# Maxout as b + relu(a-b), with the second weight cast while it loads and the early order rewritten, in a fused attention and maxout kernel

## Chip, cores and metric

The kernel runs on one core of one Trainium2 chip. The time is device microseconds of one launch, from host arrays of float32 to a float32 output. Five engines work side by side: TensorE (PE, its weight loads as PEld), VectorE (DVE), ScalarE (ACT), GpSimd (POOL) and SyncE (SP). DMAs are issued from the queues of SP, ACT and POOL.

## The reference

```python
scores = (1 / sqrt(64)) * q @ k.T          # 8 batches, 8 heads, 576 tokens, 64 wide
scores = where(block_of(row) >= block_of(col), scores, -1e9)   # blocks of 64 tokens
attn = exp(scores - max) / (sum + 1e-9)
x = (attn @ v), heads side by side          # 4608 tokens x 512
y = maximum(x @ w1, x @ w2) @ w_out         # 512 -> 1024 -> 512
```

## The kernel before, in words

All matrix work is in bfloat16. The heads are taken in pairs (p = 0 to 31, four pairs to a batch), and two pairs make a group g (q and k of a group are loaded together by `load_qk`, lines 112 to 124, cast to bf16 by `cast`, turned on TensorE by `transposes`, lines 354 to 372). Scores of a pair stand transposed, keys on partitions; `exp` (line 402) is one ScalarE instruction that reads a score buffer in PSUM, of which there are two, and writes bf16 to `aT`. `mask` (line 407) zeroes the corners on the block diagonal, mostly on GpSimd. `av` (line 471) multiplies by v with a column of constants beside it, so that the sum of the exps comes out too, and VectorE divides (lines 493 and 494) into `xp`. `x_out` (line 511) turns the result into `xT` by TensorE and two copies; from the third batch on, `x_dma` (line 502) does so by a transposing DMA.

The maximum is split: max(x w1, x w2) = (x(w1+w2) + |x(w1-w2)|) / 2. The constant beside v is 2, which halves x. The difference `d_sb` (`diff_w`, line 161) gives h by `h_unit` (line 212): four matmuls for 128 columns of d_ff and a span of tokens, then an absolute-value reduction on VectorE into `g`. The sum `s_sb` (`sum_w`, line 165) is turned by `sT_unit` (line 233) and multiplied with w_out by `m_unit` (line 245) into the small matrix `m_sb`, so that y = x m + |h| w_out has 4 + 8 matmuls for 128 tokens (`y_unit`, line 263). The weights come in four blocks of 256 columns, in float32, by `load_w` (line 148) on GpSimd's queue: the first two into buffers of their own, the last two into those of q and k. w_out is cast to bf16 as it is loaded (`load_wo`, line 171), and so is v (`load_v`, line 134).

The order is written out by hand, and each engine's queue follows the text of the program. Up to the fourth pair (lines 573 to 664) each instruction group stands by itself; from group 2 on a loop (line 673) takes one group after another. `load_qk(..., gated=True)` writes one column of the buffer on GpSimd first, so that a load on SP's queue begins when GpSimd reaches that place. The matrix work of the second half (h, sT, M and y units) stands in one list of steps; `fill(n)` (line 338) takes steps of a summed cost n off it and `fill_of` (line 542) shares what is ready among the groups. A span of h is ready when `x_out` has set `done_tokens`. The first spans have 256 and 320 tokens, the others 512. `warm_up` runs matmuls on zeros.

On GpSimd's queue the early order before the change is: cast of the third q, masks of pair 0, weight block 2, cast of the third k (line 627), masks of pair 1, weight block 3 and both halves of w_out (lines 633 to 635), masks of pair 2, three loads of v of batch 1, the key copies `pad_keys` of pairs 4 and 5, the gates of the loads of group 3, masks of pair 3, the other loads of v, and the casts of group 3. The sums and differences stand between the divisions of the `av` calls on VectorE.

Of the kernel before, what the change touches and what calls it, by code (L numbers as in the profile page):

```python
# [14 lines left out]
def kernel(  # L15
# [10 lines left out]
    nc = tc.nc  # L26
# [54 lines left out]
    small = ctx.enter_context(tc.tile_pool(name="small", bufs=4))  # L81
    xpool = ctx.enter_context(tc.tile_pool(name="xp", bufs=3))
    raw = ctx.enter_context(tc.tile_pool(name="raw", bufs=3))
    wraw = ctx.enter_context(tc.tile_pool(name="wraw", bufs=2))
    qkn = ctx.enter_context(tc.tile_pool(name="qkn", bufs=2))
    g_pool = ctx.enter_context(tc.tile_pool(name="g", bufs=2))
    y_pool = ctx.enter_context(tc.tile_pool(name="y", bufs=4))
# [11 lines left out]
    aT_r = [ring.tile([P, 2, AW + APAD], BF16, name=f"aT{r}") for r in range(NA)]  # L99
    xT = ring.tile([P, NDM, NTOK + BLK], BF16, name="xT")  # L100
    d_sb = wpool.tile([P, NDM, d_ff], BF16, name="d_sb")
    sT_sb = wpool.tile([P, NFF, d_model], BF16, name="sT_sb")
    m_sb = wpool.tile([P, NDM, d_model], BF16, name="m_sb")
    wo_sb = wpool.tile([P, NFF, d_model], BF16, name="wo_sb")
    ident = wpool.tile([P, P], BF16, name="ident")
# [20 lines left out]
    def cast(nm, g, parts):  # L126
        t = raws[nm, g].rearrange("p s (t d) -> p t s d", d=D)
        if (nm, g) not in qk_n:
            qk_n[nm, g] = qkn.tile([P, RPP, 2, D], BF16, name=f"{nm}n")
        n = qk_n[nm, g]  # L130
        for copy, j0, j1 in parts:
            copy(out=n[:, j0:j1], in_=t[:, j0:j1])  # L132

    def load_v(b, c):
        rows = min(P, S - c * P)
        nc.gpsimd.dma_start(  # L136
            out=vv_r[b % NV][P - rows:, c, :, :D],
            in_=v[b, :, c * P:c * P + rows, :].rearrange("h p d -> p h d"),
        )
# [3 lines left out]
    wor = moe_w_out.rearrange("(c p) f -> p c f", p=P)  # L143

    WB = 256
    w_raws = {}

    def load_w(j, which=(0, 1)):
        for i in which:
            if j < 2:  # L150
                t = wraw.tile([P, NDM, WB], FP32, name=f"w{i + 1}raw")[:]
            else:
                t = raw.tile([P, 2, RPP * D], FP32, name="qk"[i] + "raw").rearrange(
                    "p a b -> p (a b)")[:, :NDM * WB].rearrange("p (c f) -> p c f", c=NDM)
            w_raws[j, i] = t
            nc.gpsimd.dma_start(out=t, in_=(w1r, w2r)[i][:, :, j * WB:(j + 1) * WB])

    s_sb = g_pool.tile([P, NFF, SPAN + BLK], BF16, name="g").rearrange(
        "p f t -> p (f t)")[:, :NDM * d_ff].rearrange("p (c f) -> p c f", c=NDM)

    def diff_w(j):
        fs = slice(j * WB, (j + 1) * WB)
        nc.vector.tensor_sub(d_sb[:, :, fs], w_raws[j, 0], w_raws[j, 1])  # L163

    def sum_w(j):
        fs = slice(j * WB, (j + 1) * WB)
        nc.vector.tensor_add(s_sb[:, :, fs], w_raws[j, 0], w_raws[j, 1])

    WH = d_model // 2

    def load_wo(i):
        ds = slice(i * WH, (i + 1) * WH)
        nc.gpsimd.dma_start(out=wo_sb[:, :, ds], in_=wor[:, :, ds])  # L173
# [11 lines left out]
    load_qk(2, (SP, None))  # L185
    make_identity(nc, ident)
    for r in range(NV):
        nc.vector.memset(vv_r[r][:, :, :, D:D + 1], 2.0)
        nc.vector.memset(vv_r[r][:BLK, NCH - 1, :, :], 0.0)
    for r in range(NA):  # L190
        nc.vector.memset(aT_r[r][:, :, AW:], 0.0)
# [11 lines left out]

    done_tokens = [0]
    g_tiles = {}

    def ABS(out, in_):
        nc.vector.tensor_reduce(  # L208
            out=out, in_=in_.unsqueeze(2), op=mybir.AluOpType.max,
            axis=mybir.AxisListType.X, apply_absolute_value=True)  # L210

    def h_unit(i, f):
        if f == 0:
            g_tiles[i] = g_pool.tile([P, NFF, SPAN + BLK], BF16, name="g")
            if carry[i]:
                end = carry[i - 1] + spans[i - 1][1]
                nc.gpsimd.tensor_copy(  # L217
                    out=g_tiles[i][:, :, :carry[i]],
                    in_=g_tiles[i - 1][:, :, end - carry[i]:end])
        g = g_tiles[i]  # L220
        t0, w = spans[i]
        m = carry[i]
        pt = ps_m.tile([P, SPAN], FP32, name="ps_h", tag="m")
        for c in range(NDM):
            nc.tensor.matmul(  # L225
                pt[:, :w], d_sb[:, c, f * P:(f + 1) * P], xT[:, c, t0:t0 + w],
                start=(c == 0), stop=(c == NDM - 1),
            )
            if c == NDM - 1:
                ABS(g[:, f, m:m + w], pt[:, :w])  # L230
            yield

    def sT_unit(j):
        pt = ps_m.tile([P, 2, NDM, P], BF16, name="ps_sT", tag="m")
        for i in range(2):
            f = 2 * j + i
            for c in range(NDM):
                nc.tensor.transpose(pt[:, i, c, :], s_sb[:, c, f * P:(f + 1) * P], ident[:])
                if i == 1 and c == NDM - 1:
                    (dve if j % 2 else act)(  # L240
                        out=sT_sb[:, 2 * j:2 * j + 2, :],
                        in_=pt.rearrange("p i c d -> p i (c d)"))
                yield

    def m_unit(i, c):
        ds = slice(i * WH, (i + 1) * WH)
        pt = ps_m.tile([P, WH], FP32, name="ps_M", tag="m")
        for f in range(NFF):
            nc.tensor.matmul(  # L249
                pt[:], sT_sb[:, f, c * P:(c + 1) * P], wo_sb[:, f, ds],  # L250
                start=(f == 0), stop=(f == NFF - 1),
            )
            if f == NFF - 1:
                (act, dve)[c % 2](out=m_sb[:, c, ds], in_=pt[:])  # L254
            yield

    def y_terms(i, s):
# [38 lines left out]
    def plan():  # L296
        def h(i, f):
            t0, w = spans[i]
            units.append((h_unit(i, f), t0 + w, w / SPAN, NDM))

        def y(i, s, last=False):
            t0, w = spans[i]
            if last:
                units.append((y_last(i, s), t0 + w, 0.333, 3 * NY))
            else:
                units.append((y_unit(i, s), t0 + w, 1.0, NY))

        for i in range(NSPAN):
            for f in range(NFF):
                h(i, f)  # L310
                if i == 0 and f == NFF - 1:
                    for n in range(NFF // 2):
                        units.append((sT_unit(n), 0, 0.3, 2 * NDM))
                if i > 2 and f % 2 == 0 and f // 2 < tiles[i - 1]:
                    y(i - 1, f // 2)
            if i == 1:
                for n in range(2 * NDM):
                    units.append((m_unit(n // NDM, n % NDM), 0, 0.5, NFF))
                for j in range(2):
# [101 lines left out]
    def burst_q1(p):  # L421
        burst(p, ((0, QCUT, 320), (1, QCUT, 192)), 384)
# [151 lines left out]

    LOW = (0, -(-QCUT // RPP))
    HIGH = (LOW[1], NP)
    warm_up(16)
# [44 lines left out]
    cast("q", 2, ((pool, 0, RPP),))  # L624
    masks_q(0)
    load_w(2)
    cast("k", 2, ((pool, 0, RPP),))
    burst_q2(1)
    x_out(1, 0, 2)
    warm_up(2)  # L630
    burst_q3(1)
    masks_q(1)
    load_w(3)
    load_wo(0)
    load_wo(1)
    fill(4)
    burst_q1(2)
    transposes("q", 2, (dve, act))()
    burst_q2(2)
    av(0, [2, 3, 4])  # L640
    diff_w(1)
    burst_q3(2)
    masks_q(2)
    for c in range(3):
        load_v(1, c)
    av(1, [2, 3, 4])
    sum_w(0)
    fill(4)
    burst_q1(3)
    transposes("k", 2, (dve, act))()  # L650
    pad_keys(4)
    pad_keys(5)
    load_qk(3, (SP, SP), gated=True)
    x_out(0, 2, NCH)
    diff_w(2)
    burst_q2(3)
    av(2, [2, 3, 4])
    sum_w(1)
    burst_q3(3)
    masks_q(3)  # L660
    for c in range(3, NCH):
        load_v(1, c)
    cast("q", 3, ((pool, 0, RPP),))
    cast("k", 3, ((pool, 0, RPP),))

    x_due = []

    def av_with(p, n):
        av(p, [0, 1])
        fill(n)  # L670
        av(p, [2, 3, 4])

    for g in range(GPB, NG):
        a, b = 2 * g, 2 * g + 1
        if x_due:
            x_out(x_due.pop())
        n = fill_of(g)
        region(tile_0(a), tile_1(a))
        if g == GPB:
            av(3, [2, 3, 4])  # L680
            fill(4)
            diff_w(3)
            x_out(1, 2, NCH)
            sum_w(2)
            sum_w(3)
            fill(4)
            n = fill_of(g)
        lo, hi = max(3, n // 18), n * 2 // 9
        for p, tiles in ((a, lambda: (tile_2(a), tile_0(b))), (b, lambda: (tile_1(b), tile_2(b)))):
            fill(hi)  # L690
            if g > GPB:
                av_with(p - LAG, lo)
                if p % 2 and x_by_dma(g - 1):
                    x_dma(g - 1)
            else:
                fill(lo)
# [8 lines left out]
        if g > GPB:  # L705
            x_due.append(g - 1)
        fill(n - 2 * (lo + hi))
    for p in range(NPAIR - LAG, NPAIR):
        if x_due:
# [43 lines left out]
```

## Time and profile before

| | |
|---|---|
| time, median of 13 runs | 272.3 us (270.1 to 274.76) |
| profiled execution: time, span | 272.3 us, 270.5 us |
| mean granted TensorE clock | 0.994 |
| busy: PE, DVE, ACT, POOL | 250.8, 138.9, 143.9, 109.5 us |
| DMA | 42.35 MB, 157 GB/s mean |
| chain that ended last | PE 78%, DMA 10%, POOL 4%, ACT 3%, DVE 2%, issue 2% |

The time of a run is a little more than the span, which goes from the first to the last instruction of the profile. Busy time of TensorE is that of pipelined matmuls, each 512 columns wide one having a mean of some 380 ns of which a part lies beside its neighbours. In a timeline the bracket at a row's end is the idle time of the engine just before that row, and what released it. "aT L408" is a mask, "kn L132" a cast of k, "d_sb L163" a difference of weights. In a row of grouped instructions the numbers behind the bar are busy us and the mean ns of one, then the idle time before them.

### The profile page before, as it was taken

What the parts mean: (1) busy time and instruction counts of PE and PEld (TensorE: products, weight loads), DVE (VectorE), ACT (ScalarE), POOL (GpSimd) and SP (SyncE); (2) the same over time, 40 slices, a digit from 0 to 9 for tenths busy, and PEclk for the clock granted to TensorE, in tenths of its full rate; (3) what the DMA queues carried; (4) which work ended last, traced back from release to release, by engine and by line L of the source; (5) the groups of instructions that cost most, each with busy time, mean ns of one, the idle gap of its engine ahead of it and who ended that gap; (6) DMA issues with size and microseconds to landing.
All of it is one profiled execution on the core that took longest, in us unless ns stands there. A gap on an engine that the chain in (4) does not pass through costs nothing.

```text
span 270.5 us, 7210 instructions
## 1 busy us (share of the span) xinstructions
PE 250.8 (93%) x2983; PEld 140.4 (52%) x2983; DVE 138.9 (51%) x299; ACT 143.9 (53%) x204; POOL 109.5 (40%) x274
## 2 busy tenths in 40 slices
PE   7694859979998899999999999999999999999995
PEld 2354546865564454646464646464555554444444
DVE  5874997444576554545464646454635344233100
ACT  2783727673778946766667666675846110101111
POOL 2974914546349637453735372637221000000000
PEclk9998899999999999999999999999999999999999
DMA  7998999869479969994998399749731512122123
GB/s 247 315 252 272 232 269 105 319 40 234 71 252 144 191 206 146 235 125 192 166 217 183 145 138 242 193 145 104 121 80 51 82 39 81 39 78 77 42 84 110
DMA packets 69729, 42.35 MB, mean 157 GB/s; under 512 B 53568, under 2 KB 56000, under 8 KB 69696
## 3 DMA queue, kind: packets, MB, share of 16 engines
q1 hardware_dynamic: 28544, 31.27, 41.4%
q0 software_dynamic: 40736, 9.96, 36.4%
q10 hardware_dynamic: 416, 0.66, 0.7%
q8 instruction: 23, 0.38, 0.6%
q14 instruction: 10, 0.08, 0.1%
HBM read 34.60 MB, written 9.44 MB: 163 GB/s over the span
## 4 chain that ended last, share of the span: by engine, by line
PE 78%; DMA 10%; POOL 4%; ACT 3%; DVE 2%; issue 2%; SPq 0%; POOLq 0%; ACTq 0%
PE ps_y L268 34%; PE ps_h L225 21%; PE ps_o L487 9%; PE ps_s L379 7%; DMA qraw<-in_q_dram 5%; DMA kraw<-in_k_dram 3%; ACT aT L403 2%; PE ps_qT L360 2%; PE ps_kT L360 2%; DMA xT<-xp 2%; PE ps_M L249 1%; POOL vv L136 1%; PE ps_y L283 1%; DVE kT L368 1%; POOL wo_sb L173 1%
## 5 line engine op out<-in xcount | busy, mean ns | idle before, releaser
L403 ACT ACTIVATE aT<-ps_s 128x1024 bf16<-128x1024 f32 (+2 forms) x100 | 95.9, 996 | 31.9 <-PE ps_s L379 31.4
L208 DVE TENSOR_REDUCE g<-ps_h 128x512 bf16<-128x512 f32 (+3 forms) x80 | 50.5, 636 | 64.4 <-PE ps_h L225 63.2
L225 PE MATMUL ps_h<-xT,d_sb 128*128 128x512 bf16 (+3 forms) x320 | 72.7, 362 | 2.1 <-DVE d_sb L163 1.4
L268 PE MATMUL ps_y<-wo_sb,g 128*128 128x512 bf16 x280 | 69.9, 379 | 0.0
L408 POOL MEMSET aT<- 64x128 bf16 x124 | 22.1, 200 | 80.2 <-ACT aT L403 79.5
L487 PEld LDWEIGHTS <-aT 128*128 128x128 bf16 x960 | 37.8, 98 | 18.8 <-POOL aT L408 3.5
L225 PEld LDWEIGHTS <-d_sb 128*128 128x128 bf16 x320 | 29.1, 99 | 30.1 <-issue 4.0
L487 PE MATMUL ps_o<-vv,aT 128*128 128x65 bf16 x960 | 40.5, 195 | 4.4 <-POOL aT L408 3.4
L273 ACT COPY y<-ps_y 128x512 f32<-128x512 f32 x31 | 18.2, 587 | 48.6 <-PE ps_y L268 45.7
L268 PEld LDWEIGHTS <-g 128*128 128x128 bf16 x280 | 25.7, 98 | 29.9 <-issue 2.6
L268 PE MATMUL ps_y<-m_sb,xT 128*128 128x512 bf16 x140 | 38.0, 379 | 1.1 <-ACT m_sb L254 1.1
L379 PE MATMUL ps_s<-qT,kT 64*128 64x64 bf16 (+6 forms) x344 | 31.6, 281 | 4.0 <-ACT aT L459 1.6
L136 POOL DMA_DIRECT2D vv<-in_v_dram x40 | 33.7, 851 | 1.6 <-issue 1.2
L494 DVE TENSOR_TENSOR xp<-ps_o,rec 128x256 bf16<-128x256 f32 (+1 forms) x64 | 31.4, 491 | 2.2
L493 DVE RECIPROCAL rec<-ps_o 128x4 f32<-128x4 f32 (+1 forms) x64 | 12.1, 189 | 36.0 <-PE ps_o L487 35.7
L368 ACT COPY qT<-ps_qT 128x576 bf16<-128x576 bf16 (+1 forms) x17 | 10.3, 614 | 22.0 <-PE ps_qT L360 22.0
L268 PEld LDWEIGHTS <-xT 128*128 128x128 bf16 x140 | 12.9, 98 | 17.3 <-issue 4.2
L132 POOL CAST qn<-qraw 128x1152 bf16<-128x1152 f32 (+1 forms) x16 | 16.9, 1058 | 10.9 <-DMA qraw<-in_q_dram 10.9
L132 POOL CAST kn<-kraw 128x1152 bf16<-128x1152 f32 (+1 forms) x15 | 17.1, 1137 | 6.4 <-DMA kraw<-in_k_dram 5.4
L379 PEld LDWEIGHTS <-kT 64*128 64x128 bf16 x344 | 12.3, 95 | 14.0 <-issue 9.1
L217 POOL COPY g<-g 128x512 bf16<-128x512 bf16 x8 | 4.9, 611 | 31.6 <-DVE g L208 30.9
L368 ACT COPY kT<-ps_kT 128x576 bf16<-128x576 bf16 x15 | 9.6, 638 | 9.1 <-PE ps_kT L360 8.5
(64 smaller groups left out, 166.0 us busy)
## 6 DMA issues: line engine op xcount, KB each, us to landing
qraw<-in_q_dram SPq DMA_DIRECT2D x16, 576.0 KB, 4.5
out_dram<-y SPq DMA_DIRECT2D x35, 256.0 KB, 2.5
kraw<-in_k_dram SPq DMA_DIRECT2D x15, 576.0 KB, 5.7
vv<-in_v_dram POOLq DMA_DIRECT2D x32, 128.0 KB, 5.8
w1raw<-in_moe_w_dram POOLq DMA_DIRECT2D x2, 512.0 KB, 7.5
w2raw<-in_moe_w_dram POOLq DMA_DIRECT2D x2, 512.0 KB, 8.3
qraw<-in_moe_w_dram POOLq DMA_DIRECT2D x2, 512.0 KB, 6.5
kraw<-in_moe_w_dram POOLq DMA_DIRECT2D x2, 512.0 KB, 7.4
```

What stands on the lines that cost most here:

```text
L132: copy(out=n[:, j0:j1], in_=t[:, j0:j1])
L136: nc.gpsimd.dma_start(out=vv_r[b % NV][P - rows:, c, :, :D], in_=v[b, :, c * P:c * P + rows, :].rearrange("h p d -> p h d"),)
L208: nc.vector.tensor_reduce(out=out, in_=in_.unsqueeze(2), op=mybir.AluOpType.max, axis=mybir.AxisListType.X, apply_absolute_value=True)
L225: nc.tensor.matmul(pt[:, :w], d_sb[:, c, f * P:(f + 1) * P], xT[:, c, t0:t0 + w], start=(c == 0), stop=(c == NDM - 1),)
L268: nc.tensor.matmul(py[:], lhs, rhs, start=(n == 0), stop=(n == len(terms) - 1),)
L273: (dve if i < 2 else act)(out=y[:], in_=py[:])
L368: (copy or copies[i])(out=t[:, p0 * RPP:p1 * RPP].rearrange("q (p j) -> q p j", j=RPP), in_=pts[i][:, :, p0:p1].rearrange("q j p -> q p j"),)
L379: nc.tensor.matmul(ps[:, hh, col:col + w], kT[r, k0:k0 + P], qT[r, q0:q0 + w], start=True, stop=True,)
L403: nc.scalar.activation(out=aT_r[p % NA][:, :, a0:a0 + w], in_=ps[:, :, :w], func=AF.Exp, scale=scale,)
L408: (eng or nc.gpsimd).memset(aT_r[p % NA][BLK:, :, a0:a0 + BLK], 0.0)
L487: nc.tensor.matmul(po[:, gi, hh, :], a[:, hh, a0:a0 + P], vv[:, c, h0 + 2 * hh, :], start=(mm == 0), stop=(mm == n_mm - 1),)
L494: nc.vector.tensor_mul(xp[:, :, ts[0]:ts[0] + n, p % 2].rearrange("q s t d -> q t s d"), po[:, :, :, :D], rec[:, :n].to_broadcast([P, n, 2 ...
```

## The change

- The maximum becomes max(a, b) = b + relu(a-b): y = relu(x(w1-w2)) w_out + x(w2 w_out). The constant beside v is 1. After h, VectorE takes a maximum with 0 (`tensor_scalar_max`) in place of the absolute-value reduction. The four sums are gone; w2 itself is turned (`bT_unit`).
- w2 is loaded as bf16 (cast by the load) into columns of `xT` that are written only from the third batch on; w1 has four buffers of its own, so the weights use no q or k buffers.
- All copies of the w2 transposes and of M are on VectorE (before: alternating with ScalarE). The transposes of a w2 block stand behind the two h units of that block in the list of steps (before: all behind the first span's h).
- The order from the fourth pair's scores to the end of group 2 is rewritten: the cast of the third k stands behind the last weight block and the masks of pair 2 on GpSimd; w_out behind that cast; all five loads of v of batch 1 in one piece behind `pad_keys` and the masks of pair 3, ahead of the gates of group 3's loads; the fourth pair's first scores ahead of the later h units; all scores of group 2 ahead of the second span's h, with the remaining differences between them; then the transposes of group 3, with fill between.

```diff
-    wraw = ctx.enter_context(tc.tile_pool(name="wraw", bufs=2))
+    wraw = ctx.enter_context(tc.tile_pool(name="wraw", bufs=4))
...
+    for j in range(d_ff // WB):
+        row, n = (1, j) if j < 3 else (3, 0)
+        t0 = 3 * S - 3 * BLK + n * NDM * WB
+        w2_sb.append(xT[:, row, t0:t0 + NDM * WB].rearrange("p (c f) -> p c f", c=NDM))
 
     def load_w(j, which=(0, 1)):
...
+        fs = slice(j * WB, (j + 1) * WB)
+        if 0 in which:
+            w1_raw[j] = wraw.tile([P, NDM, WB], FP32, name="w1raw")
+            nc.gpsimd.dma_start(out=w1_raw[j][:], in_=w1r[:, :, fs])
+        if 1 in which:
+            nc.gpsimd.dma_start(out=w2_sb[j], in_=w2r[:, :, fs])
...
-        nc.vector.tensor_sub(d_sb[:, :, fs], w_raws[j, 0], w_raws[j, 1])
-
-    def sum_w(j):
-        fs = slice(j * WB, (j + 1) * WB)
-        nc.vector.tensor_add(s_sb[:, :, fs], w_raws[j, 0], w_raws[j, 1])
+        nc.vector.tensor_sub(d_sb[:, :, fs], w1_raw[j][:], w2_sb[j])
...
-        nc.vector.memset(vv_r[r][:, :, :, D:D + 1], 2.0)
+        nc.vector.memset(vv_r[r][:, :, :, D:D + 1], 1.0)
...
-                ABS(g[:, f, m:m + w], pt[:, :w])
+                nc.vector.tensor_scalar_max(g[:, f, m:m + w], pt[:, :w], 0.0)
...
-                    (dve if j % 2 else act)(
-                        out=sT_sb[:, 2 * j:2 * j + 2, :],
+                    nc.vector.tensor_copy(
+                        out=bT_sb[:, 2 * j:2 * j + 2, :],
...
-                (act, dve)[c % 2](out=m_sb[:, c, ds], in_=pt[:])
+                nc.vector.tensor_copy(out=m_sb[:, c, ds], in_=pt[:])
...
-                if i == 0 and f == NFF - 1:
-                    for n in range(NFF // 2):
-                        units.append((sT_unit(n), 0, 0.3, 2 * NDM))
+                if i == 0 and f % 2:
+                    units.append((bT_unit(f // 2), 0, 0.25, 2 * NDM))
```

The order, in the hand-written part:

```diff
     load_w(2)
-    cast("k", 2, ((pool, 0, RPP),))
     burst_q2(1)
...
     load_w(3)
-    load_wo(0)
-    load_wo(1)
     fill(4)
     burst_q1(2)
     transposes("q", 2, (dve, act))()
     burst_q2(2)
     av(0, [2, 3, 4])
-    diff_w(1)
     burst_q3(2)
     masks_q(2)
-    for c in range(3):
-        load_v(1, c)
+    cast("k", 2, ((pool, 0, RPP),))
+    load_wo(0)
+    load_wo(1)
     av(1, [2, 3, 4])
-    sum_w(0)
-    fill(4)
     burst_q1(3)
+    burst_q2(3)
+    av(2, [2, 3, 4])
     transposes("k", 2, (dve, act))()
+    burst_q3(3)
+    masks_q(3)
     pad_keys(4)
     pad_keys(5)
+    for c in range(NCH):
+        load_v(1, c)
     load_qk(3, (SP, SP), gated=True)
     x_out(0, 2, NCH)
+    fill(2)
+    diff_w(1)
+    outs = tile_0(4), tile_1(4)
+    av(3, [2, 3, 4])
+    region(*outs)
+    x_out(1, 2, NCH)
+    fill(4)
     diff_w(2)
-    burst_q2(3)
-    av(2, [2, 3, 4])
-    sum_w(1)
-    burst_q3(3)
-    masks_q(3)
-    for c in range(3, NCH):
-        load_v(1, c)
+    fill(2)
+    region(tile_2(4), tile_0(5))
+    fill(4)
+    diff_w(3)
+    fill(2)
+    region(tile_1(5), tile_2(5))
+    fill(4)
+    fill(2)
     cast("q", 3, ((pool, 0, RPP),))
     cast("k", 3, ((pool, 0, RPP),))
...
+    n = fill_of(GPB)
+    fill(n // 2)
+    transposes("q", 3, (dve, act))()
+    pool_work(4)
+    fill(n // 3)
+    transposes("k", 3, (dve, act))()
+    pad_keys(6)
+    pad_keys(7)
+    pool_work(5)
+    fill(n - n // 2 - n // 3)
+
+    for g in range(GPB + 1, NG):
```

More of the change, by code (lines that the diff above doesn't have):

```diff
@@ L101 @@
     d_sb = wpool.tile([P, NDM, d_ff], BF16, name="d_sb")
-    sT_sb = wpool.tile([P, NFF, d_model], BF16, name="sT_sb")
+    bT_sb = wpool.tile([P, NFF, d_model], BF16, name="bT_sb")
     m_sb = wpool.tile([P, NDM, d_model], BF16, name="m_sb")
@@ L145 @@
     WB = 256
-    w_raws = {}
-    def load_w(j, which=(0, 1)):
[L149 to L159, printed above, removed]
+    w1_raw, w2_sb = {}, []
+    for j in range(d_ff // WB):
+        row, n = (1, j) if j < 3 else (3, 0)
+        t0 = 3 * S - 3 * BLK + n * NDM * WB
+        w2_sb.append(xT[:, row, t0:t0 + NDM * WB].rearrange("p (c f) -> p c f", c=NDM))
+    def load_w(j, which=(0, 1)):
+        fs = slice(j * WB, (j + 1) * WB)
[4 more added lines that the diff above has]
+            nc.gpsimd.dma_start(out=w2_sb[j], in_=w2r[:, :, fs])
     def diff_w(j):
         fs = slice(j * WB, (j + 1) * WB)
-        nc.vector.tensor_sub(d_sb[:, :, fs], w_raws[j, 0], w_raws[j, 1])
-    def sum_w(j):
-        fs = slice(j * WB, (j + 1) * WB)
-        nc.vector.tensor_add(s_sb[:, :, fs], w_raws[j, 0], w_raws[j, 1])
+        nc.vector.tensor_sub(d_sb[:, :, fs], w1_raw[j][:], w2_sb[j])
     WH = d_model // 2
@@ L205 @@
     g_tiles = {}
[L207 to L210, printed above, removed]
     def h_unit(i, f):
@@ L229, in h_unit, with bT_unit @@
             if c == NDM - 1:
-                ABS(g[:, f, m:m + w], pt[:, :w])
+                nc.vector.tensor_scalar_max(g[:, f, m:m + w], pt[:, :w], 0.0)
             yield
-    def sT_unit(j):
-        pt = ps_m.tile([P, 2, NDM, P], BF16, name="ps_sT", tag="m")
+    def bT_unit(j):
+        pt = ps_m.tile([P, 2, NDM, P], BF16, name="ps_bT", tag="m")
         for i in range(2):
-            f = 2 * j + i
             for c in range(NDM):
-                nc.tensor.transpose(pt[:, i, c, :], s_sb[:, c, f * P:(f + 1) * P], ident[:])
+                nc.tensor.transpose(pt[:, i, c, :], w2_sb[j][:, c, i * P:(i + 1) * P], ident[:])
                 if i == 1 and c == NDM - 1:
-                    (dve if j % 2 else act)(
-                        out=sT_sb[:, 2 * j:2 * j + 2, :],
+                    nc.vector.tensor_copy(
+                        out=bT_sb[:, 2 * j:2 * j + 2, :],
                         in_=pt.rearrange("p i c d -> p i (c d)"))
@@ L249, in m_unit @@
             nc.tensor.matmul(
-                pt[:], sT_sb[:, f, c * P:(c + 1) * P], wo_sb[:, f, ds],
+                pt[:], bT_sb[:, f, c * P:(c + 1) * P], wo_sb[:, f, ds],
                 start=(f == 0), stop=(f == NFF - 1),
@@ L573, in t_pair, with av_with @@
         return lambda: [f() for f in outs]
+    x_due = []
+    def av_with(p, n):
+        av(p, [0, 1])
+        fill(n)
+        av(p, [2, 3, 4])
     LOW = (0, -(-QCUT // RPP))
@@ L640 @@
     av(0, [2, 3, 4])
-    diff_w(1)
     burst_q3(2)
     masks_q(2)
-    for c in range(3):
-        load_v(1, c)
+    cast("k", 2, ((pool, 0, RPP),))
+    load_wo(0)
+    load_wo(1)
     av(1, [2, 3, 4])
-    sum_w(0)
-    fill(4)
     burst_q1(3)
+    burst_q2(3)
+    av(2, [2, 3, 4])
     transposes("k", 2, (dve, act))()
+    burst_q3(3)
+    masks_q(3)
     pad_keys(4)
     pad_keys(5)
+    for c in range(NCH):
+        load_v(1, c)
     load_qk(3, (SP, SP), gated=True)
     x_out(0, 2, NCH)
-    diff_w(2)
-    burst_q2(3)
-    av(2, [2, 3, 4])
-    sum_w(1)
-    burst_q3(3)
-    masks_q(3)
-    for c in range(3, NCH):
-        load_v(1, c)
+    fill(2)
[5 more added lines that the diff above has]
+    fill(4)
+    diff_w(2)
+    fill(2)
[6 more added lines that the diff above has]
+    fill(2)
     cast("q", 3, ((pool, 0, RPP),))
     cast("k", 3, ((pool, 0, RPP),))
[L666 to L673, printed above, removed]
+    n = fill_of(GPB)
[9 more added lines that the diff above has]
+    for g in range(GPB + 1, NG):
         a, b = 2 * g, 2 * g + 1
@@ L678 @@
         region(tile_0(a), tile_1(a))
[L679 to L687, printed above, removed]
         lo, hi = max(3, n // 18), n * 2 // 9
@@ L690 @@
             fill(hi)
[L691 to L696, printed above, removed]
+            av_with(p - LAG, lo)
+            if p % 2 and x_by_dma(g - 1):
+                x_dma(g - 1)
             copy_out = t_pair(p)
@@ L704 @@
             pool_work(p)
-        if g > GPB:
-            x_due.append(g - 1)
+        x_due.append(g - 1)
         fill(n - 2 * (lo + hi))
```

## Prediction

> **What bounds the kernel now.** I read the page's engine totals first, then the busy times by stretch, the timelines of TensorE and GpSimd, the chain that ended last, and the groups of instructions by shape.
>
> ```profile
> PE 250.8 (93%) x2983; PEld 140.4 (52%) x2983; DVE 138.9 (51%) x299; ACT 143.9 (53%) x204; POOL 109.5 (40%) x274
> ```
>
> TensorE is the bound: 250.8 us busy. The change leaves it the same matrix work (32 transposes of 128x128 for w2 in place of 32 for w1+w2, the same h, M, y, scores and AV), so only its idle time and its clock can change. The busy times by stretch (us, then each engine's busy time with its instructions, granted clock, DMA share, GB/s) say where that is.
>
> ```profile
> 21.70:25.10 3.40, 0.03 (x1) 0.00 (x0) 0.94 (x2) 1.26 (x2) 1.38 (x3) 1.00 1.03 348
> 25.10:28.50 3.40, 3.38 (x36) 2.48 (x38) 2.80 (x5) 0.00 (x0) 3.23 (x5) 0.53 0.56 181
> ...
> 100.00:264.00 164.00, 163.91 (x1677) 85.42 (x1676) 72.45 (x148) 79.78 (x114) 52.68 (x138) 1.00 0.65 124
> ```
>
> From 100 us on TensorE never waits (163.91 of 164.00), while VectorE is busy 72.45. What the change does there, a max with 0 in place of an absolute-value reduction on VectorE, is worth nothing either way; what TensorE gains before 100 us stays gained to the end. The 3.40 us from 21.70 hold no matmul, and in the 3.40 us behind them the granted clock is 0.53. The timeline of TensorE names its waits in the stretch that the change rewrites.
>
> ```profile
> 18.61 1.11 PE L225 MATMUL ps_h<-xT,d_sb 128*128 128x256 bf16 x8
> ...
> 25.12 1.29 PE L487 MATMUL ps_o<-vv,aT 128*128 128x65 bf16 x22 [3.39 <-POOL aT L408]
> 30.31 0.88 PE L487 MATMUL ps_o<-vv,aT 128*128 128x65 bf16 x24 [0.68 <-ACT kT L368]
> ...
> 31.96 0.40 PE L379 MATMUL ps_s<-qT,kT 64*128 64x64 bf16 x4 [0.33 <-ACT aT L403]
> ...
> 36.06 1.05 PE L225 MATMUL ps_h<-xT,d_sb 128*128 128x256 bf16 x8 [1.45 <-DVE d_sb L163]
> 36.94 1.06 PE L238 MATMUL ps_sT<-ident,g 128*128 128x128 bf16 x16
> 38.66 1.08 PE L238 MATMUL ps_sT<-ident,g 128*128 128x128 bf16 x16 [0.65 <-ACT sT_sb L240]
> ...
> 41.13 0.44 PE L360 MATMUL ps_qT<-ident,qn 64*128 64x64 bf16 x18 [1.26 <-POOL qn L132]
> 41.40 0.22 PE L397 MATMUL ps_s<-qT,kz 64*128 64x64 bf16 x4
> 41.46 0.57 PE L379 MATMUL ps_s<-qT,kT 64*128 64x320 bf16 x6
> 41.97 2.48 PE L225 MATMUL ps_h<-xT,d_sb 128*128 128x320 bf16 x17
> ...
> 56.11 0.89 PE L487 MATMUL ps_o<-vv,aT 128*128 128x65 bf16 x24 [0.35 <-ACT m_sb L254]
> 60.72 0.59 PE L268 MATMUL ps_y<-m_sb,xT 128*128 128x512 bf16 x2 [1.14 <-ACT m_sb L254]
> ```
>
> **Part 1, the cast of the third k moves (the 3.39 us).** The wait is for masks on GpSimd; its timeline shows what stood ahead of them, and the chain that ended last what that waited for.
>
> ```profile
> 23.66 1.15 POOL L132 CAST kn<-kraw 128x1152 bf16<-128x1152 f32 x1 [5.04 <-DMA kraw<-in_k_dram]
> 24.86 0.34 POOL L408 MEMSET aT<- 64x128 bf16 x2
> ...
> 26.85 1.79 POOL L173 DMA_DIRECT2D wo_sb<-in_moe_w_out_dram  x2
> ...
> 28.90 2.67 POOL L136 DMA_DIRECT2D vv<-in_v_dram  x3
> ```
> ```profile
> 14.20 9.31 DMA kraw<-in_k_dram
> ...
> 32.21 7.57 DMA qraw<-in_q_dram
> ```
> ```profile
> 17.02 2.32 ACT L403 ACTIVATE aT<-ps_s 128x1024 bf16<-128x1024 f32 x3
> ...
> 21.53 1.43 ACT L403 ACTIVATE aT<-ps_s 128x1024 bf16<-128x1024 f32 x2
> ```
>
> The k lands at 23.51 (14.20 + 9.31); until then GpSimd stands in front of the cast, and the masks of pair 1, whose exps were done at 19.34 (17.02 + 2.32), run at 24.86. After the change nothing stands ahead of them: masks of pair 1 at 19.4, the two issues of the last weight block to 21.2, masks of pair 2 when their exps end at 22.96 (21.53 + 1.43), about 23.3, and only then the cast, at 23.66 as before. So AV of pair 1 runs from 21.5, without the wait. With that gap goes the slow clock: 3.40 us at 0.53 is 3.40 x 0.47 = 1.6 us of matrix work lost. What is late next is the cast itself: the transposes of this k now stand right behind AV of pair 2.
>
> **Part 2, the new order, walked through.** Durations come from the grouped instructions by shape.
>
> ```profile
> L403 ACT ACTIVATE aT<-ps_s 128x1024 bf16<-128x1024 f32 x92 | 91.2, 1026 | 30.6 <-PE ps_s L379 30.1
> ...
> L494 DVE TENSOR_TENSOR xp<-ps_o,rec 128x384 bf16<-128x384 f32 x32 | 17.8, 558 | 1.1
> ...
> L368 DVE COPY kT<-ps_kT 128x576 bf16<-128x576 bf16 x15 | 11.2, 749 | 0.1
> ...
> L493 DVE RECIPROCAL rec<-ps_o 128x6 f32<-128x6 f32 x32 | 6.3, 195 | 13.0 <-PE ps_o L487 12.7
> ...
> L208 DVE TENSOR_REDUCE g<-ps_h 128x256 bf16<-128x256 f32 x8 | 3.1, 418 | 0.5 <-PE ps_h L225 0.5
> ...
> L163 DVE TENSOR_TENSOR d_sb<-w1raw,w2raw 128x1024 bf16<-128x1024 f32 x2 | 2.4, 1220 | 2.5 <-DMA w2raw<-in_moe_w_dram 2.5
> ...
> L254 DVE CAST m_sb<-ps_M 128x256 bf16<-128x256 f32 x4 | 1.7, 419 | 2.6 <-PE ps_M L249 2.6
> ...
> L240 DVE COPY sT_sb<-ps_sT 128x1024 bf16<-128x1024 bf16 x2 | 1.3, 682 | 0.0
> ...
> L531 DVE COPY xT<-ps_xo 128x256 bf16<-128x256 bf16 x3 | 0.8, 282 | 0.0
> L530 DVE COPY xT<-ps_xe 128x384 bf16<-128x384 bf16 x2 | 0.7, 350 | 0.0
> ```
>
> TensorE: AV of pair 1 21.5 to 22.3; first and second scores of pair 3 when the two exps free their buffers (22.55 and 22.96), to 23.3; AV of pair 2 to 24.15 (0.8 each: the rows have 0.88, whose tail lies under the next group); then the cast's end, 24.81 (23.66 + 1.15), is waited for: 0.7 lost. Transposes of k, last scores of pair 3, x transposes of group 0 and one w2 transpose unit (half of the 16-step row, 0.45) take it to 26.15. The first scores of pair 4 then wait briefly for kT (VectorE copy to 26.0) and the second for a buffer; AV of pair 3 waits for its masks, which stand behind the two wo issues (1.79 behind the cast: 26.6, masks done 26.95), and ends at 27.75.
>
> From there VectorE's queue decides. It holds, in order: kT copy to 26.0, two xT copies (0.35 + 0.28) to 26.6, w2 transpose copy (0.68) to 27.3, second subtraction (1.22) to 28.5, the divide of AV 3 (0.20 + 0.56) to 29.25. The x transposes of group 1 therefore start at 29.35, 1.6 lost. They and h 2 and 3 (0.9 for two units) end at 30.6, the next w2 transposes and scores (0.45 + 0.57) at 31.6. VectorE meanwhile: xT copies to 30.4, two maxima of 0.42 to 31.25, third subtraction to 32.45; h 4 and 5 start at 32.5, 0.9 lost, and end at 33.4. Next w2 copy and two maxima take VectorE to 34.0, the last subtraction to 35.2; TensorE is through with w2 transposes and the last scores of group 2 at 34.4 and starts h 6 and 7 at 35.25, 0.85 lost. With the last w2 transposes it stands at h of the second span at 36.6.
>
> The kernel before stands there at 42.05: its scores row begins the second span's h at 41.97, one early h step (0.2) and the q transposes (0.28) are to be taken off that, and the second half of group 2's scores (0.57) has to be added, since the new order has done it already. Gain to this point: 42.05 - 36.6 = 5.45 us. The four sums w1+w2 (1.22 each) are gone from VectorE in this; without that they would have stood in the same queue.
>
> **Part 3, copies.** All eight M copies go to VectorE (0.42) instead of half behind ScalarE's exps of 1.03. The 0.35 and 1.14 at 56.11 and 60.72 go; the last M copy still has to end before the first y, some 0.6. Gain 0.9. The w2 transpose copies on VectorE are in the walk.
>
> **Part 4, the loads.**
>
> ```profile
> 24.66 1.22 DVE L163 TENSOR_TENSOR d_sb<-w1raw,w2raw 128x1024 bf16<-128x1024 f32 x1 [2.46 <-DMA w2raw<-in_moe_w_dram]
> ```
> ```profile
> w2raw<-in_moe_w_dram POOLq DMA_DIRECT2D x2, 512.0 KB, 8.3
> ...
> wo_sb<-in_moe_w_out_dram POOLq DMA_DIRECT2D x2, 512.0 KB, 10.6
> ```
>
> No w2 load that casts is in this trace. wo is the nearest: it casts, writes 512 KB and lands in 10.6 us; a w2 block then writes half of that. Its landing lies between half of 8.3 (half the bytes written) and 10.6, so 4.2 us earlier to 2.3 later; I take no change, as it reads what it read. The second block was waited for until 24.66 and is now wanted at 27.3, which leaves 2.6 for the 2.3; the third follows it in the queue and is wanted at 31.25, the fourth, issued by 21.2, at 34.0. The five v loads now stand in one piece ahead of the loads of group 3: GpSimd is through with masks and keys at 27.5, needs 5 x 0.89 for them (2.67 for three), and the q load starts at 32.1, where it starts now (32.21). Since the last weight block no longer waits behind the cast, the queue ahead of it is shorter by the hole at 25 us (DMA share 0.56 instead of 1.03 for 3.40 us, 1.6 us). TensorE wants this q only after 16 units of fill, at about 40.1, when its cast, at 39.8 + 1.15 at the latest, should be nearly done. I take 0, bounds 0 to +1.
>
> The Trainium skill, "DMA: Bandwidth & Descriptors", section "Queues, rings and completion order", says that each DMA engine takes turns between queues packet by packet. By that rule smaller packets of a casting w2 load would let the third k, on another queue, land before 23.51, and the sum would be up to 0.7 better (265.3); no row here shows it.
>
> **Sum.** 5.45 + 0.9 = 6.3 us. The profiled execution took 272.3 us for a span of 270.5, and 272.3 is also the median of the 13 runs: 272.3 - 6.3 = 266.0. Within this walk the walk's own error (0.1 per handover on VectorE, some ten of them, either way) and the load bounds make 264.5 to 268.
>
> **Rivals.** *The loads set the pace (0.20).* TensorE comes 5 us earlier to group 3, and q and k of groups 3 and 4 may not: the q load of group 3 starts at the same 32.1. For it: the 1.26 wait at 41.13 is such a wait already, and DMA was at a share over 1 around it. Against: after 41.13 TensorE waits for no cast again. Then 1 us goes at group 3's transposes and up to 2 at group 4's: 269.0, to 271. *VectorE's queue is shorter than I walk it (0.12).* The three waits of 1.6, 0.9 and 0.85 make 3.35; if instructions overlap as back-to-back ones do, half goes: 264.3, all of it 262.7. *Slower, the third k lands late (0.05).* It is now straight on TensorE's path: from 23.5 each us of landing is a us of the end, and the gain is gone at 23.5 + 6.3 = 29.8. For it: 9.31 us of landing, with three more blocks queued beside it. Against: these queue in order behind blocks already there. Landing at 31 would make 273.5. *Slower, w2 in xT ties things together (0.03).* If the first h, which reads columns of xT, waited for all w2 blocks (about 29) instead of running at 18.61, some 10 us and a slow clock came in for the 10.8 of waits and clock lost now (3.39, 1.6, 0.68, 0.33 for a score buffer, 1.45, 0.65, 1.26, 0.35, 1.14) and a rest of VectorE's waits: 275. Against: the columns do not overlap.
>
> **How the numbers follow.** My walk has 0.60. A measurement of this kernel tells 0.5%, 1.4 us, from no change. The walk, the shorter queue and three quarters of the load case are faster by more: 0.60 + 0.12 + 0.15 = 0.87; the rest of the load case is the same, 0.05; the last two are slower, 0.08. The range goes from half of VectorE's waits gone and a little more, 263.4, to most of the load case, 270.0; outside lie the slower cases, the worst of the load case and the best of the queue case, together under 0.2.
>
> **What would show it.** Right: no wait of TensorE for masks near 21.7, clock 1.0 from 25 to 28.5; a wait under 1 us for the k cast near 24.2; waits for VectorE (xp, d_sb) near 28, 32 and 34.5; h of the second span starting near 36.6; no wait for ScalarE's m_sb. Wrong: k landing after 26, waits at the transposes of groups 3 and 4 over 1 us, or new waits after 50 us.

## The result, and the profile after

| | before | after |
|---|---|---|
| median | 272.84 us (270.1 to 274.76, 48 runs) | 264.99 us (264.64 to 266.25, 11 runs) |
| ratio | | 0.9733, 95% interval 0.9708 to 0.9757 |
| span of the profiled execution | 270.5 us | 263.3 us |
| mean granted TensorE clock | 0.994 | 1.0 |
| busy PE, DVE, ACT, POOL | 250.8, 138.9, 143.9, 109.5 us | 249.4, 137.4, 140.9, 109.5 us |

The kernel is 7.85 us faster by the medians of the table, 7.3 by the ratio (2.67% of 272.84) and 7.2 by the spans of the two profiled executions. The same stretches of the timeline as before the change, and the steady part (us, busy time of PE, PEld, DVE, ACT and POOL with their instructions, granted clock, DMA share, GB/s):

```profile
21.70:25.10 3.40, 2.83 (x79) 2.17 (x76) 2.04 (x6) 3.30 (x5) 2.24 (x4) 1.00 1.24 319
25.10:28.50 3.40, 2.31 (x47) 1.73 (x47) 3.23 (x7) 2.69 (x4) 3.30 (x8) 1.00 1.32 229
100.00:257.00 157.00, 157.00 (x1595) 81.66 (x1592) 69.07 (x141) 75.36 (x107) 48.49 (x126) 1.00 0.65 126
```

The 3.40 us from 21.70 that held no matmul hold 2.83 us of them, and the clock stays at 1.00. From 100 us TensorE is busy without a gap, as it was. The timeline of TensorE, with its waits in brackets, in the stretch that was rewritten:

```profile
21.47 0.91 PE L475 MATMUL ps_o<-vv,aT 128*128 128x65 bf16 x24
22.61 0.78 PE L367 MATMUL ps_s<-qT,kT 64*128 64x320 bf16 x10 [0.23 <-ACT aT L391]
23.32 0.90 PE L475 MATMUL ps_o<-vv,aT 128*128 128x65 bf16 x24
24.46 0.44 PE L348 MATMUL ps_kT<-ident,kn 64*128 64x64 bf16 x18 [0.25 <-POOL kn L132]
...
25.66 0.61 PE L227 MATMUL ps_bT<-ident,xT 128*128 128x128 bf16 x8 [0.24 <-ACT kT L356]
...
28.91 0.20 PE L513 MATMUL ps_xe<-ident,xp 64*128 64x64 bf16 x1 [1.25 <-DVE xp L482]
...
31.88 1.05 PE L215 MATMUL ps_h<-xT,d_sb 128*128 128x256 bf16 x8 [0.63 <-DVE d_sb L162]
...
34.58 1.05 PE L215 MATMUL ps_h<-xT,d_sb 128*128 128x256 bf16 x8 [0.60 <-DVE d_sb L162]
...
35.91 3.69 PE L215 MATMUL ps_h<-xT,d_sb 128*128 128x320 bf16 x26
40.13 0.44 PE L348 MATMUL ps_qT<-ident,qn 64*128 64x64 bf16 x18 [0.52 <-POOL qn L132]
```

AV of pair 1 runs at 21.47 without a break. The waits that are left make 0.23 + 0.25 + 0.24 + 1.25 + 0.63 + 0.60 + 0.52 = 3.72 us. Before, the waits of this part made 3.39 + 0.68 + 0.33 + 1.45 + 0.65 + 1.26 + 0.35 + 1.14 = 9.25, and the slow clock 1.6 on top: 10.85. The difference, 7.1, is nearly that of the spans, 7.2; the waits between 62 and 100 us, which both kernels have, make 2.9 before and 3.0 after. GpSimd's timeline shows the cast in its new place:

```profile
22.61 0.20 POOL L396 MEMSET aT<- 64x128 bf16 x1 [1.51 <-ACT aT L391]
23.00 0.20 POOL L396 MEMSET aT<- 64x128 bf16 x1 [0.18 <-ACT aT L391]
23.26 1.15 POOL L132 CAST kn<-kraw 128x1152 bf16<-128x1152 f32 x1
...
38.93 1.14 POOL L132 CAST qn<-qraw 128x1152 bf16<-128x1152 f32 x1 [2.79 <-DMA qraw<-in_q_dram]
```

It has no wait for a DMA any more: the k had landed when the masks of pair 2 were through.

### The profile page after: what moved, and what is told of

The parts are those of the page before. It is cut to its first block, busy times and chain, and to the rows that moved or that the text cites. A ratio compares the mean times of both kernels' runs of the same rounds, so it can differ in the third digit from the quotient of the medians.

```text
span 263.3 us, 7204 instructions
## 1 busy us (share of the span) xinstructions
PE 249.4 (95%) x2983; PEld 139.6 (53%) x2983; DVE 137.4 (52%) x301; ACT 140.9 (53%) x198; POOL 109.5 (42%) x274
## 4 chain that ended last, share of the span: by engine, by line
PE 84%; DMA 7%; POOL 3%; ACT 3%; DVE 1%; issue 1%; ACTq 0%; POOLq 0%
PE ps_y L257 36%; PE ps_h L215 21%; PE ps_o L475 10%; PE ps_s L367 7%; DMA qraw<-in_q_dram 5%; PE ps_M L238 3%; PE ps_qT L348 2%; ACT aT L391 2%; PE ps_kT L348 2%; DMA xT<-xp 2%; POOL vv L136 1%; PE ps_w L337 1%; PE ps_y L272 1%; PE ps_s L385 1%; ACT qT L356 1%
## 5 line engine op out<-in xcount | busy, mean ns | idle before, releaser
L220 DVE TENSOR_SCALAR g<-ps_h 128x512 bf16<-128x512 f32 (+3 forms) x80 | 50.6, 636 | 64.1 <-PE ps_h L215 62.2
L215 PE MATMUL ps_h<-xT,d_sb 128*128 128x512 bf16 (+3 forms) x320 | 71.7, 358 | 2.0 <-DVE d_sb L162 1.2
L475 PEld LDWEIGHTS <-aT 128*128 128x128 bf16 x960 | 37.2, 98 | 14.0 <-issue 2.2
L475 PE MATMUL ps_o<-vv,aT 128*128 128x65 bf16 x960 | 39.7, 194 | 0.0
```

The costliest lines, as they stand in the source:

```text
L215: nc.tensor.matmul(pt[:, :w], d_sb[:, c, f * P:(f + 1) * P], xT[:, c, t0:t0 + w], start=(c == 0), stop=(c == NDM - 1),)
L220: nc.vector.tensor_scalar_max(g[:, f, m:m + w], pt[:, :w], 0.0)
L475: nc.tensor.matmul(po[:, gi, hh, :], a[:, hh, a0:a0 + P], vv[:, c, h0 + 2 * hh, :], start=(mm == 0), stop=(mm == n_mm - 1),)
```

## The experiments

My theory: TensorE's early waits are a row of late things of which the masks behind the cast were the first, so that no part brings its price alone, and what is left is VectorE's queue from 25 to 36 us. The rivals: the cast's place is the gain; or the lighter VectorE work and casting loads carry it and the order is worth little. Times are medians; each ratio is to the kernel before on the same chip, so runs from different chips are better compared by their ratios. No run has uncast loads of w2 in the new order, or the old absolute-value reduction in it: what these two are worth by themselves is not measured.

| run | median us | ratio, 95% interval |
|---|---|---|
| e1_cast_only | 272.51 | 1.0008 (0.9968 to 1.0048) |
| e2_cast_back | 267.15 | 0.9795 (0.9737 to 0.9854) |
| e3_h_first | 268.67 | 0.9862 (0.9811 to 0.9913) |
| e4_adds | 267.82 | 0.9821 (0.9777 to 0.9866) |
| e5_m_act | 265.21 | 0.9718 (0.9683 to 0.9753) |
| e6_bt_act | 266.46 | 0.9750 (0.9700 to 0.9801) |
| e7_qk_early | 264.08 | 0.9678 (0.9642 to 0.9713) |
| e8_both | 264.40 | 0.9692 (0.9658 to 0.9727) |
| e9_bt_behind | 264.04 | 0.9686 (0.9644 to 0.9728) |
| e10_diff_early | 264.26 | 0.9689 (0.9649 to 0.9730) |
| e11_all | 263.53 | 0.9675 (0.9631 to 0.9720) |
| after_again | 265.16 | 0.9730 (0.9689 to 0.9770) |

**The move of the cast alone**, in the kernel before:

```diff
     load_w(2)
-    cast("k", 2, ((pool, 0, RPP),))
...
     masks_q(2)
+    cast("k", 2, ((pool, 0, RPP),))
     for c in range(3):
```

> The kernel before with one thing changed: the cast of the third k stands behind the masks of pair 2 on GpSimd. Theory (the mask wait is one of several late things, and behind it stands the wait for the second weight block on VectorE until 24.66 us plus a subtraction of 1.22): AV of pair 1 runs at 21.5, then h 2 and 3 wait from about 22.3 to 25.9, the clock drops again, and the whole gains 1 to 2.5 us: 270 to 272. Rival (the cast's place is the gain): 3.4 us of wait and 1.6 of clock go, 267.8.

TensorE's timeline of this run:

```profile
21.41 0.91 PE L487 MATMUL ps_o<-vv,aT 128*128 128x65 bf16 x24
25.99 1.89 PE L225 MATMUL ps_h<-xT,d_sb 128*128 128x256 bf16 x8 [3.68 <-DVE d_sb L163]
...
36.22 1.05 PE L225 MATMUL ps_h<-xT,d_sb 128*128 128x256 bf16 x8 [1.45 <-DVE d_sb L163]
...
41.08 0.44 PE L360 MATMUL ps_qT<-ident,qn 64*128 64x64 bf16 x18 [1.06 <-POOL qn L132]
```

The wait of 3.39 for masks is gone, and one of 3.68 for the second weight difference stands in its place; the matmuls behind it take 1.89 for eight, so the clock drops as before. In this execution it even stays low longer, 0.50 from 26 to 31 us, where before it was 1.00 from 29 us on. Ratio 1.0008, and its interval leaves room for 0.3% at most, 0.9 us: less than the 1 to 2.5 I gave it. The second wait for a difference (1.45) is as it was, and at the q transposes of group 3 the kernel stands at 41.08 where it stood at 41.13: the cast of that q starts at 39.88, before at 39.93. The rival that the cast's place is the gain is out.

**The cast put back**, in the changed kernel:

```diff
     load_w(2)
+    cast("k", 2, ((pool, 0, RPP),))
     burst_q2(1)
...
     masks_q(2)
-    cast("k", 2, ((pool, 0, RPP),))
```

> The changed kernel with the cast of the third k back behind weight block 2, ahead of the masks of pair 1 and of weight block 3. Theory: AV of pair 1 waits from 21.5 to about 24.7 for its masks, the slow clock comes back, and some of the later waits for VectorE hide part of it: 3 to 5 us lost, 268 to 270. The cast's start shows when this k lands beside the casting loads (23.51 before). Rival (the rest of the new order carries the gain): under 1.5 us lost, below 266.5.

TensorE's wait, then the pieces of the chain that ended last around the k load:

```profile
24.16 0.85 PE L475 MATMUL ps_o<-vv,aT 128*128 128x65 bf16 x22 [2.20 <-POOL aT L396]
```
```profile
14.13 8.42 DMA kraw<-in_k_dram
22.55 0.03 issue
```

By the medians 2.2 us are lost (267.15 against 264.99), fewer than the 3 to 5 expected; by the spans of the profiles 1.3 (264.6 against 263.3). In the profiled execution the k lands in 8.42 us instead of 9.31, and after a gap of 2.20 the clock stays at 1.00, so no slow matmuls follow. The four timed runs fall into two pairs: 265.55 and 266.33 with a mean granted clock of 1.000, 267.98 and 268.12 with 0.994, which is also the mean of the profiled execution before, with its one slow stretch. So what the gap costs seems to depend on whether the clock drops behind it (of the second pair no trace is kept), and the median lies between the pairs. With so few runs the rival (under 1.5 us) is not out: the interval of the ratio, 0.9737 to 0.9854, still overlaps that of the changed kernel, 0.9708 to 0.9757. What the trace does show is that in the new order the wait for the masks comes back, 2.20 us, when the cast is put back.

**The second block's h first again**, in the changed kernel:

```diff
+    diff_w(1)
     av(1, [2, 3, 4])
+    fill(2)
+    fill(4)
     burst_q1(3)
...
     x_out(0, 2, NCH)
-    fill(2)
-    diff_w(1)
...
     x_out(1, 2, NCH)
-    fill(4)
     diff_w(2)
```

> The changed kernel with the first w2 transposes and h 2 and 3 ahead of the fourth pair's first scores again, with their subtraction ahead of the division of AV 1. Theory: they wait for the second weight block, from about 22.8 to 25.5 or 26, and later waits of VectorE (1.25, 0.63, 0.60 us in the changed kernel) shrink: 1 to 2.5 us lost, 266 to 267.5. Rival (the weight blocks now land so early that this order costs nothing): within 0.7 of 265.0.

TensorE's wait, the subtraction on VectorE that it waits for, and two stretches of 2 us around it:

```profile
25.49 1.52 PE L215 MATMUL ps_h<-xT,d_sb 128*128 128x256 bf16 x8 [2.72 <-DVE d_sb L162]
```
```profile
23.89 1.55 DVE L162 TENSOR_TENSOR d_sb<-w1raw,xT 128x1024 bf16<-128x1024 f32 x1 [1.76 <-DMA xT<-in_moe_w_dram]
```
```profile
23.00:25.00 2.00, 0.00 (x0) 0.00 (x0) 1.11 (x1) 0.00 (x0) 1.94 (x3) 1.00 1.30 282
25.00:27.00 2.00, 1.51 (x10) 0.91 (x12) 1.97 (x5) 0.00 (x0) 1.05 (x2) 0.73 1.30 269
```

3.7 us lost, more than expected, because the clock drops after a gap of 2.72 already. The subtraction starts only when the weight block has landed, at 23.89: that is not early enough for this order even with the casting loads, so placing h 2 and 3 behind the fourth pair's first scores is a gain of its own. The interval of the ratio lies clear above that of the changed kernel.

**VectorE's work put back**, in the changed kernel, as three additions to a spare buffer that nothing reads:

```diff
         nc.vector.tensor_sub(d_sb[:, :, fs], w1_raw[j][:], w2_sb[j])
+        if j:
+            nc.vector.tensor_add(spare[:], w1_raw[j][:], w2_sb[j])
```

> The changed kernel with an addition of w1 and w2 (128x1024, as the sums before) to a spare buffer behind each of the last three subtractions: VectorE work of the size that the change took away. Theory (VectorE's queue sets the pace from 27 to 36 us): the waits for xp and for the two d_sb grow by 1.1 each for the first two and by little for the third, 2 to 3 us lost, 267 to 268. Rival (VectorE has slack): within 0.7 of 265.0.

TensorE's timeline:

```profile
30.77 0.20 PE L516 MATMUL ps_xe<-ident,xp 64*128 64x64 bf16 x1 [2.40 <-DVE xp L485]
...
38.11 1.05 PE L218 MATMUL ps_h<-xT,d_sb 128*128 128x256 bf16 x8 [0.79 <-DVE d_sb L163]
```

2.8 us lost. The wait for xp grows from 1.25 to 2.40, by 1.15, the one addition ahead of it. Behind the longer gap the clock is 0.52 from 31 to 33 us, so part of the 2.8 is slow clock and not VectorE's queue itself; in the slow stretch the first of the two waits for d_sb goes, and the second is 0.79. The wait for xp shows that VectorE's queue is the pace there, and the interval, clear of the changed kernel's, that the sums that the change took away were worth having away.

**M copies alternating again**, in the changed kernel:

```diff
-                nc.vector.tensor_copy(out=m_sb[:, c, ds], in_=pt[:])
+                (act, dve)[c % 2](out=m_sb[:, c, ds], in_=pt[:])
```

> The changed kernel with the M copies alternating between ScalarE and VectorE again. Theory of the prediction (the engine of the copies is worth 0.9 us): waits of TensorE for m_sb come back, 265.5 to 266.5. Rival (in the new order ScalarE stands idle at most of these moments, so the copies were late before only because of where the exps stood): within 0.4 of 265.0 and no wait for m_sb over 0.3 us.

ScalarE of this run, then of the kernel before, around the last of its M copies:

```profile
51.78 0.37 ACT L243 CAST m_sb<-ps_M 128x256 bf16<-128x256 f32 x1
...
53.74 1.95 ACT L391 ACTIVATE aT<-ps_s 128x1024 bf16<-128x1024 f32 x2
```
```profile
58.03 1.95 ACT L403 ACTIVATE aT<-ps_s 128x1024 bf16<-128x1024 f32 x2
...
60.30 0.37 ACT L254 CAST m_sb<-ps_M 128x256 bf16<-128x256 f32 x1
```

265.21, no change, and TensorE waits for no m_sb. The rival holds: three of the four copies find ScalarE idle, and the last stands ahead of the two exps from 53.74. Before, the last stood behind the two exps from 58.03, and TensorE waited 1.14 for it. The exps around these copies are the same as before, three pairs of them; what moved is where the M units end between them. The engine of these copies is worth nothing.

**Copies of the w2 transposes on ScalarE, the gates ahead of the loads of v, and both**, in the changed kernel:

```diff
-                    nc.vector.tensor_copy(
+                    act(
                         out=bT_sb[:, 2 * j:2 * j + 2, :],
```

> The changed kernel with all four copies of the w2 transposes on ScalarE. Theory (VectorE's queue sets the pace from 27 to 36 us, each copy being 0.68 of it): the waits of 1.25, 0.63 and 0.60 us shrink to some 0.6, 0 and 0.2, 1 to 1.7 us gained: 263.3 to 264. Rival (the copies of 1.01 us on ScalarE delay exps as much, or VectorE is not the bound): within 0.4 of 265.0.

```diff
-    for c in range(NCH):
-        load_v(1, c)
     load_qk(3, (SP, SP), gated=True)
+    for c in range(NCH):
+        load_v(1, c)
```

> The changed kernel with the gates of group 3's q and k loads ahead of the five loads of v. Theory: the loads start at about 27.2 instead of 31.3, the wait of 0.52 us for the q cast goes, and nothing else moves: 0.5 gained, 264.5. Rival (the load case of the prediction: the DMAs are full, and what q and k gain v loses): v of batch 1 lands after 46.5, and AV of pair 4 waits: 265 or more.

> Both: copies of the w2 transposes on ScalarE, and the gates ahead of the loads of v. If both theories hold they add up, since the q cast would otherwise be wanted earlier: 1.5 to 2.3 us gained, 262.7 to 263.5. If the second span's h starts earlier but q still lands at the same time, the first gain is lost again at the q transposes of group 3 in the run without the gates moved, and only this one shows it.

TensorE of e6_bt_act, then GpSimd and VectorE of it, and last the q cast of e7_qk_early on GpSimd:

```profile
28.59 0.20 PE L513 MATMUL ps_xe<-ident,xp 64*128 64x64 bf16 x1 [0.88 <-DVE xp L482]
...
41.02 0.44 PE L348 MATMUL ps_qT<-ident,qn 64*128 64x64 bf16 x18 [1.69 <-POOL qn L132]
```
```profile
26.61 1.13 POOL L374 COPY kz<-kT 128x128 bf16<-128x128 bf16 x2
27.69 0.88 POOL L136 DMA_DIRECT2D vv<-in_v_dram  x1
```
```profile
26.14 1.21 DVE L162 TENSOR_TENSOR d_sb<-w1raw,xT 128x1024 bf16<-128x1024 f32 x1
```
```profile
36.15 1.14 POOL L132 CAST qn<-qraw 128x1152 bf16<-128x1152 f32 x1
```

The copies on ScalarE (e6_bt_act) did not gain: 266.46, its interval around that of the changed kernel. The wait for xp shrank from 1.25 to 0.88 and one d_sb wait went, as expected, but the wait for the q cast grew from 0.52 to 1.69. Part of it is that TensorE asks earlier; part is GpSimd. Without the copy ahead of it the second subtraction starts at 26.14 and lies over the two key copies, which take 1.13 us instead of 0.53 in the changed kernel; behind them stand the five loads of v and the gate.

With the gates moved alone the q cast starts at 36.15 instead of 38.93, TensorE no longer waits for it, and the median is 264.08, 0.9 better than the changed kernel (interval 0.9642 to 0.9713 against 0.9708 to 0.9757, which just overlap). 0.52 of it is that wait. In the profiles another 0.6 lies at 88 to 90 us, where h waits for the transposing DMA of xp: 0.60 and 0.16 in the changed kernel, 0.17 here. But a second profile of the changed kernel (after_again, span 262.3) has 0.16 there too, so this part comes and goes with the execution. AV of pair 4 waits for no v, so the rival is out. Both together, 264.40, are no better than the gates alone: the 1.5 to 2.3 expected did not come. The waits on VectorE are smaller there as in e6_bt_act, but a score buffer, freed later by an exp behind a copy, costs 0.35.

**VectorE's order instead of its engine**, with the gates moved:

```diff
     x_out(0, 2, NCH)
-    fill(2)
     diff_w(1)
...
     region(*outs)
+    fill(2)
     x_out(1, 2, NCH)
```

> The kernel with the gates moved ahead of the loads of v, and besides the first w2 transposes behind AV of pair 3 instead of ahead of the second subtraction; no engine changes. Theory (the order on VectorE's queue makes the 1.25 us wait for xp): the subtraction and with it the division of AV 3 come 0.4 to 0.6 us earlier, TensorE has the transposes to do in the meantime, the wait shrinks to 0.6 to 0.9: 0.4 to 0.6 gained against the run with the gates moved (264.1), about 263.6. The subtraction then runs beside the key copies of GpSimd, which took 0.90 instead of 0.30 us beside one in the runs with copies on ScalarE; that delays the q load by 0.6, which it can bear here. Rival: the slower key copies or a score buffer cost as much, 264 or more.

```diff
     x_out(1, 2, NCH)
+    diff_w(2)
     fill(4)
-    diff_w(2)
     fill(2)
     region(tile_2(4), tile_0(5))
+    diff_w(3)
     fill(4)
-    diff_w(3)
     fill(2)
```

> The kernel with the gates moved, and besides the third and fourth subtraction one fill earlier, ahead of the maxima of the h units before. Theory: the two waits of TensorE for d_sb (0.63 and 0.60) go, since the blocks have long landed, and nothing is late in their place but a PSUM buffer for a tenth or two: 0.9 to 1.2 gained against 264.1, about 263.0. Rival: the maxima come 1.2 later each and hold the h units' PSUM buffers, and TensorE waits for those instead: 263.7 to 264.3.

> All three orders together (gates, first w2 transposes, third and fourth subtraction). If VectorE's queue order is what is left of the waits between 25 and 36 us, the gains add: 1.3 to 1.8 against 264.1, 262.3 to 262.8. If not, no better than the better of the two single ones.

> The changed kernel as it is, beside the three others on the same chip: 265.0, 0.971 to 0.976 of the kernel before.

TensorE of e11_all:

```profile
24.51 0.44 PE L348 MATMUL ps_kT<-ident,kn 64*128 64x64 bf16 x18 [0.24 <-POOL kn L132]
...
28.22 0.20 PE L513 MATMUL ps_xe<-ident,xp 64*128 64x64 bf16 x1 [0.44 <-DVE xp L482]
...
32.87 0.23 PE L385 MATMUL ps_s<-qT,kz 64*128 64x64 bf16 x4 [0.56 <-ACT aT L391]
...
34.56 3.69 PE L215 MATMUL ps_h<-xT,d_sb 128*128 128x320 bf16 x26
```

From the k transposes to the second span's h TensorE needs 34.56 - 24.51 = 10.05 us, in the changed kernel 35.91 - 24.46 = 11.45, and with the gates alone the same 11.45. e9_bt_behind needs 10.72 and e10_diff_early 10.77, so in the profiles the two orders add up (0.73 and 0.68 make 1.41; 1.40 measured). The xp wait is 0.44 instead of 1.25 and both d_sb waits are gone, for a score-buffer wait of 0.56. In the timed runs less of it is seen: 264.04 and 264.26 alone, expected at 263.6 and 263.0, are not to be told from 264.08, and 263.53 together, expected at 262.3 to 262.8, is 0.5 better than the gates alone, within the intervals. So the gain of these orders is read from the profiles and not shown in the time. The wait for the transposing DMA near 88 us blurs it: 0.57 in the profile of e9_bt_behind, 1.18 in that of e10_diff_early, none in that of e11_all. By the median e11_all is the fastest version tried: 0.9675 of the kernel before, and 1.6 us under the changed kernel timed beside it (265.16), where the intervals still overlap.

## Why the prediction was right, point by point

266.0 was forecast and 264.99 measured. Against its own starting time the profile moved by 7.2 us where 6.3 were forecast: the second span's h came 0.7 earlier than walked and the M copies brought 0.6 more, and a wait for the q cast took 0.5 of that back.

- **The mask wait and the clock** (Part 1): as walked. AV of pair 1 stood at 21.5 in the walk and runs at 21.47; the clock is 1.00 from 25 to 28.5. What the walk had right is that the cast's move needs the order behind it; e1_cast_only shows that without it the weight block takes over at once. The mean granted clock of the timed runs is 0.998 to 1.0 after the change; in the runs of the kernel before that were timed beside the experiments it is 0.981 to 0.994.
- **The wait for the k cast**: 0.7 forecast, 0.25 measured, since the k lands earlier: 8.2 us from issue to landing in the changed kernel, 8.42 in e2_cast_back, 9.31 before. In the last two the same loads are queued beside it up to there, except that w2 is cast as it loads. DMA packets between 14 and 24 us were 3403 before and 4318 in e2_cast_back, the added ones under 2 KB. The rule that I set beside this, from the Trainium skill, "DMA: Bandwidth & Descriptors", section "Queues, rings and completion order" (each engine takes turns packet by packet), agrees with the direction; of the 0.7 that I had set as its most, the wait shrank by 0.45. That the packets are the cause, and not the halved bytes that a w2 load writes, was argued and not tried by itself.
- **VectorE's queue**: the waits stood in the walk at 1.6, 0.9 and 0.85, and are 1.25, 0.63 and 0.60, with the same releasers in the same order. The difference, 0.87, is in part the earlier k (its copy on VectorE ends at 25.71, walked at 26.0) and in part the overlap of back-to-back instructions, which I had left to the bounds: in this queue each starts some 0.08 before the one ahead of it ends (the next copy starts at 25.62). The rival of a shorter queue was true for a quarter of the 3.35. h of the second span starts at 35.91, forecast 36.6. e4_adds shows that this queue is the pace, and the profiles of e9 to e11 agree.
- **The copies of M** (Part 3): 0.9 forecast, and the waits of 0.35 and 1.14 did go, without the 0.6 that I charged for the last copy: TensorE runs into y without a break, 1.5 gained. But the reason was wrong, and that a gain came here was luck. e5_m_act has the copies where they were, and no wait comes back: what the rows there show instead is the new place of the M units between the exps, which was not varied by itself.
- **The loads** (Part 4): 0 forecast with bounds 0 to 1; 0.52 measured at the q cast of group 3. The load rival was there in small: e7_qk_early gets it back with the gates ahead of the loads of v. At group 4's transposes nothing waits.
- **The slower rivals**: the k did not land late, and the first h does not wait for columns of xT; it runs at 18.59.

## What to carry to other kernels

When TensorE waits for something late, look up what it would wait for next if that were on time, before you price the move: here the first wait's removal alone was worth nothing that ten runs could show, since the next late thing stood right behind it. Then read the queue of the engine that hands over (here VectorE) entry by entry, and put first the entry that the bound engine asks for first. Moving work to an idle engine is not the same: a copy moved to ScalarE cleared VectorE and let a subtraction slide over GpSimd's copies, which started the loads later.

## What the runs showed of the hardware that I had not expected

The clock drops after shorter gaps than the 3.39 us of the kernel before. With TensorE idle for 2.72 us (e3_h_first) it is 0.73 in the two microseconds around the restart and 0.50 in the next two, and with 2.40 us (e4_adds) 0.52 from 31 to 33 us; with 2.20 us (e2_cast_back) it stayed at 1.00 in the profiled execution. Where the limit lies is not shown: two of the timed runs of e2_cast_back have a mean of 0.994, as e3_h_first and e4_adds have in their profiles, which leaves open that it drops behind this gap in them. The row of e4_adds:

```profile
31.00:33.00 2.00, 2.00 (x18) 1.43 (x12) 1.01 (x4) 0.00 (x0) 1.42 (x6) 0.52 1.41 183
```

A VectorE instruction that reads two operands from SBUF held up GpSimd copies from SBUF: of the two key copies in e6_bt_act one took 0.90 us beside the subtraction that ran from 26.14 to 27.35, and both took 0.30 in the changed kernel, where the subtraction began at 26.91, when the second of them, the last, was already running. The Trainium skill, "SBUF — State Buffer", section "SBUF: two separate sides", says that the two engines share a port pair that one of them holds for a whole instruction; these times agree with it.
